# Scores of the last query chunk of images two to four in half as many products, and the second head mixing one step later

## The chip, the cores and the metric

The kernel runs on one core of a Trainium2 chip. The metric is the device time of one execution in microseconds (us). Engines are named as the profile names them: PE multiplies matrices (PEld loads its weights), DVE, ACT and POOL work on elements, SP issues most of the transfers.

## The reference, cut to what matters

```python
def _attn_ref(q, k, v, w_pre, w_post):          # 4 images, 12 heads, 448 rows, 64 wide
    scores = scale * np.matmul(q, k.transpose(0, 1, 3, 2))
    scores = np.einsum('bhij,hg->bgij', scores, w_pre)       # first mixing of heads
    scores = scores - np.max(scores, axis=-1, keepdims=True)
    attn = np.exp(scores)
    attn = attn / (np.sum(attn, axis=-1, keepdims=True) + 1e-09)
    attn = np.einsum('bhij,hg->bgij', attn, w_post)          # second mixing
    return np.matmul(attn, v)

def _moe_ref(x, w_gate, w_val, w_out, rms_g):   # x is 1792 x 768, d_ff 1536
    xn = x / np.sqrt(np.mean(x * x, axis=-1, keepdims=True) + 1e-06) * rms_g
    g = xn @ w_gate
    return g * (1.0 / (1.0 + np.exp(-g))) * (xn @ w_val) @ w_out
```

## The kernel before

The kernel has two parts, one after the other. The **attention** (`part_a`) is a loop of 92 steps, followed by some steps that finish what is left. The **gated layer** (`part_b`) is a long row of f16 products on PE. The change is in the attention alone.

The 448 query rows of an image are cut into four chunks (`NC`), and a chunk `n` (0 to 15 over the four images) into six, six, six and five steps (`PAIRS`). A step is a pair `(n, p)` and handles 20 query rows (10 in the last step of an image). Four kinds of products on PE serve it:

- **scores** (`qk_mm`, tiles `qk`, L140): 64x64 weights cut from `q`, 448 columns of `k`. One call makes the scores of two heads for the whole chunk, in four products, into two PSUM banks of `ps_q`. In `qk`, the row half of the array (which head of the pair) goes with the bank. Six calls make a chunk, and one call stands in each step until they run out. They run about a chunk and a half ahead of the steps that use them.
- ACT and DVE copy the two banks to tiles `st` (`qk_evac`, L162 and L160), and one transfer per head (`r<-st`, L179, on SP's queue) gathers the rows into `r`, where 12 heads of 5 rows stand in 60 partitions. There are three buffers `r`.
- **first mixing** (`premix`, tiles `sp`, L187): the 64x64 weights `wk_pre` on `r`, into two banks of `ps_s`. DVE takes the row maximum (`rowmax`, `nm`, L196), ACT the exponential with its row sum (`expo`, `e`, L203). `norm` adds 1e-9 (`t`, DVE, L210), takes the reciprocal (`rp`, DVE, L212) and scales the second mixing's weights with it (`wn`, POOL, L215).
- **second mixing** (`postmix`, tiles `pm`, L226): 28 products with `e` as weights and `wn` moving. In step t it works on the pair of step t-1 (`back(1)`). ACT and DVE copy its two banks into `at_all` (`evac_a`, L265 and L263).
- **attention times values** (`av_mm`, tiles `av`, L294) of finished chunk pairs, a part of 16 instructions of the trace per head pair, one or two parts in a step. ACT copies the result to `xt`, POOL squares and adds it (`x_sum`), and once per image PE sums the columns of these squares (`sq_all`, tile `pss`, L347) for the later normalization; the scores' second bank is lent for that.

Nothing is planned by a cost model: the order on each engine is that of the calls in the loop, and tables (`qk_at`, `av_at`, `jobs_at`, `last_at`) say in which step which call stands. On PE a step reads: `sp` of one half, `qk` of one bank, `sp` of the other half, `qk` of the other bank, then `pm`, then `av`. On DVE it reads: two maxima, one `st` copy, one `at_all` copy, `t`, `rp`. In steps 23 to 78 DVE also converts weights of the gated layer (`first_w`, tiles `wac`). Scores of chunk 15 end in step 84, so steps 85 to 91 have none.

Of the kernel before, what the change touches and what calls it, by code (L numbers as in the profile page):

```python
# [7 lines left out]
F32 = mybir.dt.float32  # L8
# [16 lines left out]
GROUPS = [12, 12, 12, 9]  # L25
# [26 lines left out]
def attention_moe(ctx: ExitStack, tc, q, k, v, wpre, wpost, mask, ident, wgv, wo, rms_g, out):  # L52
# [33 lines left out]
    wk_pre = cst.tile([128, 64], F32, name="wk_pre")  # L86
    wk = cst.tile([128, HR], F32, name="wk")

    msk = pro.tile([128, 2, RH], F32, name="msk", tag="ksm1")
    we = pro.tile([128, H], F32, name="we", tag="ksm2")  # L90
    wp = pro.tile([128, H], F32, name="wp", tag="ksm3")

    def load_consts():
        nc.sync.dma_start(msk.rearrange("p a r -> p (a r)"), mask)
        nc.sync.dma_start(we, wpre)
        nc.sync.dma_start(wp, wpost)

    def setup():
        nc.vector.tensor_scalar(we, we, D ** -0.5, None, ALU.mult)
        nc.vector.memset(wk_pre, 0.0)  # L100
        for i, (o, w) in enumerate(((wk_pre[:, :HR], we), (wk, wp))):
# [10 lines left out]
    def load_q(n, hp, many=3, eng=nc.gpsimd):  # L112
        b, c = divmod(n, NC)
        if not hp:
            qt[n] = pq.tile([128, H // 2, 128], F32, name=f"q{n}", tag="q", bufs=2)
        hp = slice(hp, hp + many)
        eng.dma_start(qt[n][:, hp], q[b, :, c, hp])
# [8 lines left out]
    held = []  # L126
# [7 lines left out]
    def qk_mm(n, hp):  # L134
# [6 lines left out]

        return [[lambda j=j, u=u: one(j, u) for u in range(2)] for j in range(2)]
# [8 lines left out]

    def qk_evac(n, hp, j):
        h, np_ = 2 * hp + j, PAIRS[n % NC]
        ps = qps[n, hp][j]
        if n == 0 and h < 1 or n == 1 and h < 2 * AHEAD:
            st = pro.tile([128, S], F32, name="st", tag="st", bufs=11)
        else:
            st = pq.tile([128, S], F32, name="st", tag="st", bufs=12)
        if j:
            nc.vector.tensor_copy(st, ps[:, :S])  # L160
        else:
            nc.scalar.activation(st, ps[:, :S], AF.Copy)  # L162
        for i, (lo, hi) in enumerate(((0, EARLY), (EARLY, 2 * np_)) if n == 0 else ((0, GROUPS[n % NC]),)):
            w, at_ = RH * (hi - lo), 2 * RH * lo
            if h < H - 1:
                parts = [(h, 2 * RH, at_, 2 * w)]
            else:
                parts = [(h, RH, at_, w), (64, RH, at_ + w, w)]
            for row, k_, src, many in parts:
                dst = rt[n][row : row + (k_ - 1) * GAP + 1 : GAP, lo:hi]  # L170
                if i:
                    held.append((dst, st[src : src + many]))
                else:
# [1086 lines left out]
```

## Time and profile before

| what | us |
|---|---|
| median of 3 runs | 827.72 (825.3 to 830.05) |
| the profiled execution | 822.48 |
| its span, first to last instruction | 820.6 |
| up to the first step of the attention loop | 20.1 |
| attention loop, to the first product of the gated layer | 308.5 |
| the rest | 492.0 |

In the views below, a row of the timeline gives the start in the span, the length, engine, line, operation, the tiles (written <- read), the shape and how many instructions are merged; idle time before it and what ended it stand in brackets. A fp32 product of PE stands as two instructions, so the 4 products of `sp` in a step are x8. A row of the waits gives who waited <- for whom: us in total, times, longest. A row of the stretches gives, behind the length, the busy time of PE, PEld, DVE, ACT and POOL with the number of instructions, the granted share of PE's clock, the busy share of the transfer engines and GB/s. PE's busy time says little here: an instruction counts from its start to its modelled end, and up to four run beside each other in the quarters of the array.

### The profile page before, as it was taken

How to read it: one execution, taken by the hardware profiler on the slowest of the kernel's cores; microseconds unless marked ns; L12 is line 12 of the kernel's file. 1: busy time of each engine (PE TensorE's matmuls, PEld its weight loads, DVE VectorE, ACT ScalarE, POOL GpSimd, SP SyncE). 2: the span in 40 equal slices, each digit the busy share in tenths (PEclk: the TensorE clock that was granted, in tenths of full speed). 3: DMA queues.
4: the chain of work that ended last, by engine and by line, in shares of the span. 5: the costliest groups of instructions: out<-in, count | busy, mean ns of one | idle time of the engine just before them, and what ended most of it. 6: DMA issues, size and time to landing. Idle time of an engine off the chain costs nothing.

```text
span 820.6 us, 26914 instructions
## 1 busy us (share of the span) xinstructions
PE 794.4 (97%) x10806; PEld 485.2 (59%) x10806; DVE 634.5 (77%) x1322; ACT 507.3 (62%) x1133; POOL 350.4 (43%) x467
## 2 busy tenths in 40 slices
PE   7899999999999989899999999999999999999998
PEld 2567777767776767655555555555555555555555
DVE  5777878888798867888788978997889676547562
ACT  3677778777776867664344454545444546969850
POOL 7212343454355435843624433426144359452310
PEclk9999999999999999999999999999999999999999
DMA  7777777777876754564255644754546446566641
GB/s 216 208 216 217 219 229 222 228 219 232 222 234 200 211 147 150 158 230 118 66 177 150 183 129 127 216 149 121 174 145 201 133 127 184 157 199 176 184 135 67
DMA packets 81902, 145.15 MB, mean 177 GB/s; under 512 B 10527, under 2 KB 72797, under 8 KB 81779
## 3 DMA queue, kind: packets, MB, share of 16 engines
q1 hardware_dynamic: 79982, 139.83, 57.0%
q0 software_dynamic: 832, 2.06, 1.0%
q8 instruction: 85, 1.39, 0.7%
q10 hardware_dynamic: 965, 1.56, 0.6%
q14 instruction: 38, 0.31, 0.1%
HBM read 72.83 MB, written 31.88 MB: 128 GB/s over the span
## 4 chain that ended last, share of the span: by engine, by line
PE 86%; DMA 8%; DVE 2%; issue 1%; ACT 1%; POOL 1%; SPq 0%; ACTq 0%; DVEq 0%; POOLq 0%
PE qk L140 7%; PE pm L226 7%; PE sp L187 7%; PE av L294 6%; PE pg L750 6%; PE pg L752 6%; PE pv L752 6%; PE pg L751 6%; PE pv L751 6%; PE pv L750 6%; DMA r<-st 6%; PE po L751 6%; PE po L750 6%; PE po L752 6%; DMA wraw<-in_wgv 1%
## 5 line engine op out<-in xcount | busy, mean ns | idle before, releaser
L187 PE MATMUL sp<-r,wk_pre 64*64 64x448 f32 x720 | 167.4, 542 | 5.4 <-DMA r<-st 3.5
L203 ACT ACTIVATE e<-sp,nm 128x448 f32<-128x448 f32 x180 | 114.3, 637 | 84.8 <-DVE nm L196 82.4
L140 PE MATMUL qk<-k,q 64*64 64x448 f32 x768 | 152.6, 559 | 5.9 <-DMA q<-in_q 4.1
L196 DVE TENSOR_REDUCE nm<-sp 128x1 f32<-128x448 f32 x180 | 110.3, 620 | 44.1 <-PE sp L187 27.4
L215 POOL TENSOR_SCALAR wn<-wk,rp 128x60 f32<-128x60 f32 x180 | 59.5, 345 | 181.8 <-DVE rp L212 109.7
L226 PEld LDWEIGHTS pm<-wn,e 60*64 60x64 f32 x5040 | 106.1, 134 | 37.6 <-POOL wn L215 23.8
L226 PE MATMUL pm<-wn,e 60*64 60x60 f32 x5040 | 106.7, 220 | 4.2 <-issue 4.1
L798 POOL TENSOR_TENSOR sg<-sg,u 128x448 f32<-128x448 f32 x36 | 45.9, 1275 | 151.2 <-ACT sg L795 106.7
L294 PE MATMUL av<-at_all,v 64*64 64x240 f32 (+6 forms) x1728 | 93.6, 316 | 4.6 <-issue 2.6
L750 PE MATMUL pv<-x,wh 128*128 128x448 f16 x264 | 93.0, 352 | 0.0
L752 PE MATMUL pv<-x,wl 128*128 128x448 f16 x264 | 93.0, 352 | 0.0
L752 PE MATMUL pg<-x,wl 128*128 128x448 f16 x264 | 93.0, 352 | 0.0
L751 PE MATMUL pv<-x,wh 128*128 128x448 f16 x264 | 93.0, 352 | 0.0
L751 PE MATMUL pg<-x,wh 128*128 128x448 f16 x264 | 93.0, 352 | 0.0
L750 PE MATMUL pg<-x,wh 128*128 128x448 f16 x264 | 93.0, 352 | 0.0
L750 PE MATMUL po<-h,fac 128*128 128x448 f16 (+1 forms) x258 | 89.8, 348 | 0.0
L751 PE MATMUL po<-h,fac 128*128 128x448 f16 (+1 forms) x258 | 89.8, 348 | 0.0
L752 PE MATMUL po<-h,fac 128*128 128x448 f16 (+1 forms) x258 | 89.8, 348 | 0.0
L750 PEld LDWEIGHTS <-wh 128*128 128x128 f16 x528 | 51.7, 98 | 48.2 <-issue 0.2
L751 PEld LDWEIGHTS <-wh 128*128 128x128 f16 x528 | 51.7, 98 | 48.3 <-issue 0.3
L752 PEld LDWEIGHTS <-wl 128*128 128x128 f16 x528 | 51.7, 98 | 48.2
L187 PEld LDWEIGHTS sp<-r,wk_pre 64*64 64x64 f32 x720 | 60.3, 133 | 27.2 <-ACT e L203 13.2
(167 smaller groups left out, 1567.3 us busy)
## 6 DMA issues: line engine op xcount, KB each, us to landing
r<-st SPq DMA_DIRECT2D x117, 210.0 KB
hraw<-td SPq DMA_DIRECT2D x84, 224.0 KB
wraw<-in_wgv SPq DMA_DIRECT2D x20, 768.0 KB
td<-keep SPq DMA_DIRECT2D x48, 224.0 KB
wraw<-in_wo SPq DMA_DIRECT2D x12, 768.0 KB
r<-st SPq DMA_DIRECT2D x44, 157.5 KB
v<-in_v SPq DMA_DIRECT2D x24, 256.0 KB
k<-in_k SPq DMA_DIRECT2D x24, 224.0 KB
```

The lines of the kernel that those rows point to most:

```text
L140: nc.tensor.matmul(ps[j][m, :S], qt[n][sl, hp, m], kt[n // NC, hp][sl], start=True, stop=True)
L187: nc.tensor.matmul(o, wk_pre[sl], rt[n][sl, 2 * p + v_], start=True, stop=True)
L196: nc.vector.tensor_reduce(t, ps[:, :S], AX.X, ALU.max, negate=True)
L203: nc.scalar.activation(e, ps[:, :S], AF.Exp, bias=nmx.pop((n, p, u)), accum_out=sm[n, p][:, u : u + 1])
L215: nc.gpsimd.tensor_scalar(wn[n, p][:, u], wk, r[:, u : u + 1], 1.0, ALU.mult, ALU.mult)
L226: nc.tensor.matmul(o[:, :, at_], e_[sl, j : j + JT], w_[sl].rearrange("p (s i) -> p s i", s=2), start=True, stop=True)
L294: nc.tensor.matmul(x, vt[b, hp][sl, j, c_], a, start=(c_ == 0), stop=(c_ == JC - 1))
L750: nc.tensor.matmul(ps, a, xh[:, kk, at_], start=(kk == 0), stop=False)
L751: nc.tensor.matmul(ps, a, xl_[:, kk, at_], start=False, stop=False)
L752: nc.tensor.matmul(ps, a2, xh[:, kk, at_], start=False, stop=(kk == KT - 1))
L798: nc.gpsimd.tensor_tensor(h, sg, u, ALU.mult)
```

## The change

- In images two to four the fourth chunk (chunks 7, 11, 15; `shared`) has fewer rows of its own: the other three chunks carry 8 rows of it each, in the 8 places of 128 that they had free, and the fourth keeps 60 rows per head. Its scores take three calls instead of six, each for four heads with 64 rows. The four products of a call are the same in size; two of them, of the two row halves, now write the same bank.
- The scores' schedule is compressed: a chunk starts one step after the chunk two before it has begun. Steps 34, 35, 57, 58 and 80 to 84 have no scores now.
- The `st` tiles become one tile `st_all` of 12 parts (`st_1` for chunk 1). After every third call (half a chunk) a small transfer (`rest_out`) takes the extra rows to a new tile `rest`, 12 rows of four stored per half chunk in place of the gather; a shared chunk issues four at once, of 12 rows each. The first and the last step of a shared chunk read `rest` with a second set of weights `wk_pre[:, 1]`.
- The second mixing stands two steps behind the first, up to step 84; step 85 makes two of them, and from there on it is one step behind as before. The values products start one step later with it, up to chunk 11.
- In `norm`, adding 1e-9 goes from DVE to POOL (except for the last chunk).
- The column sums of images one to three move from steps 40, 63 and 84 to steps 57, 79 and 84.

```diff
-    for i, a in enumerate([(n, hp) for n in range(1, NCHUNK) for hp in range(H // 2)][AHEAD:]):
-        qk_at[i].append(a)
+    starts, t_ = {}, -1
+    for n in range(1, NCHUNK):
+        for hp in range(H // 4 if shared(n) else H // 2):
+            if n == 1 and hp < AHEAD:
+                continue
+            t_ = max(t_ + 1, first[n - 2] + 1 if n > 1 else 0)
+            starts.setdefault(n, t_)
+            qk_at[t_].append((n, hp))
+    mix_at = [[] for _ in range(T + 40)]
+    near = first[14] + 4
+    for i, step in enumerate(steps):
+        mix_at[i + 2 if i < near - 2 else max(i + 1, near)].append(step)
...
+        def two(j, i):
+            sl, u = slice(64 * j, 64 * j + 64), (i + j) % 2
+            nc.tensor.matmul(ps[i][64 * u : 64 * u + 64, :S], qt[n][sl, 2 * hp + i], kt[n // NC, 2 * hp + i][sl], start=True, stop=True)
+
+        if shared(n):
+            return [[lambda j=j, i=i: two(j, i) for j in (i, 1 - i)] for i in range(2)]
...
+    def rest_out(n, half, st):
+        if shared(n):
+            for i in range(2):
+                for u in range(2):
+                    rows = slice(100 + 12 * u, 112 + 12 * u)
+                    nc.sync.dma_start(rest[rows, slot(n - 3 + i)], st[64 * u + 60 + 2 * i : 64 * u + 62 + 2 * i, :6])
+        else:
+            nc.sync.dma_start(rest[4 + half : 4 + half + 95 : 2, slot(n)], st[120:, 6 * half : 6 * half + 6])
...
-        nc.vector.tensor_scalar(t, s, 1e-9, None, ALU.add)
+        (nc.gpsimd if n < NCHUNK - 1 else nc.vector).tensor_scalar(t, s, 1e-9, None, ALU.add)
...
-        t = first[NC * b + NC + 2] + (5 if b < B - 2 else 3)
-        for i in range(17):
-            last_at[t + max(i - 2, 0) // 3].append((sq_all, b, i))
-        chain(t, lambda b=b: x_scale_ops(b), 2 if b < B - 2 else 4)
+        t = (first[10] - 1, first[13] + 4, first[14] + 3)[b]
+        for i in range(16):
+            last_at[t + (max(i - 1, 0) if i < 4 else 3 + (i - 4) // 3)].append((sq_all, b, i))
+        chain((first[6] + 8, first[10] + 6, first[14] + 3)[b], lambda b=b: x_scale_ops(b), 1 if b < B - 2 else 4)
...
-            if back(1):
-                postmix(*back(1))
+            for a in mix_at[t]:
+                postmix(*a)
+                if a is not mix_at[t][-1]:
+                    for v_ in range(2):
+                        evac_a(*a, v_)
```

PE in steps 34 and 35 before (the last step of chunk 5 and the first of chunk 6; `qk` are scores of chunk 7):

```order
L187 MATMUL sp<-r_123,wk_pre 64x448 x2
L140 MATMUL qk<-k_3_1036,q_2195 64x448 x2
L187 MATMUL sp<-r_123,wk_pre 64x448 x2
L140 MATMUL qk<-k_3_1036,q_2195 64x448 x2
L226 MATMUL pm<-wn,e 64x2x30 x28
L294 MATMUL av<-at_all,v_2_1337 64x220 x8
L187 MATMUL sp<-r_121,wk_pre 64x448 x2
L140 MATMUL qk<-k_4_1104,q_2195 64x448 x2
L187 MATMUL sp<-r_121,wk_pre 64x448 x2
L140 MATMUL qk<-k_4_1104,q_2195 64x448 x2
L226 MATMUL pm<-wn,e 64x2x30 x28
```

And PE in the same two steps now, up to the first product of step 36:

```order
L232 MATMUL sp<-r_126,wk_pre 64x448 x4
L271 MATMUL pm<-wn,e 64x2x30 x28
L339 MATMUL av<-at_all,v_1_1099 64x220 x4
L339 MATMUL av<-at_all,v_1_1099 64x2x55 x4
L232 MATMUL sp<-r_124,wk_pre 64x448 x4
L271 MATMUL pm<-wn,e 64x2x30 x28
L339 MATMUL av<-at_all,v_2_1251 64x220 x8
L232 MATMUL sp<-r_124,wk_pre 64x448 x2
```

The eight score products are gone from the two steps, and the values products stand one step later.

PE in steps 84 and 85 before, the fourth and fifth of chunk 14, with the column sums of image three at the end of step 84:

```order
L187 MATMUL sp<-r_123,wk_pre 64x448 x2
L140 MATMUL qk<-k_5_5062,q_6111 64x448 x2
L187 MATMUL sp<-r_123,wk_pre 64x448 x2
L140 MATMUL qk<-k_5_5062,q_6111 64x448 x2
L226 MATMUL pm<-wn,e 64x2x30 x28
L294 MATMUL av<-at_all,v_2_6272 64x240 x12
L294 MATMUL av<-at_all,v_2_6272 64x2x60 x4
L347 MATMUL pss<-ones,sum_5224 112x1 x4
L187 MATMUL sp<-r_123,wk_pre 64x448 x4
L226 MATMUL pm<-wn,e 64x2x30 x28
L294 MATMUL av<-at_all,v_3_6429 64x240 x12
L294 MATMUL av<-at_all,v_3_6429 64x2x60 x4
```

And PE in the same two steps now:

```order
L232 MATMUL sp<-r_126,wk_pre 64x448 x4
L271 MATMUL pm<-wn,e 64x2x30 x28
L339 MATMUL av<-at_all,v_1_5881 64x240 x4
L339 MATMUL av<-at_all,v_1_5881 64x2x60 x4
L339 MATMUL av<-at_all,v_2_6041 64x240 x8
L392 MATMUL pss<-ones,sum_5109 112x1 x4
L232 MATMUL sp<-r_126,wk_pre 64x448 x4
L271 MATMUL pm<-wn,e 64x2x30 x56
L339 MATMUL av<-at_all,v_2_6041 64x240 x4
L339 MATMUL av<-at_all,v_2_6041 64x2x60 x4
L339 MATMUL av<-at_all,v_3_6199 64x240 x12
L339 MATMUL av<-at_all,v_3_6199 64x2x60 x4
```

Step 85 now has two second mixings in a row, which write the same two banks, and three parts of values products behind them.

DVE in one step of image two before, from one pair of maxima to the next:

```order
L196 TENSOR_REDUCE nm<-sp 128x1 x2
L160 COPY st<-qk 128x448
L263 COPY at_all<-pm 128x2x42x5
L210 TENSOR_SCALAR t<-s 128x2
L212 RECIPROCAL rp<-t 128x2
```

DVE in such a step now, with the conversion that follows it there:

```order
L241 TENSOR_REDUCE nm<-sp 128x1 x2
L194 COPY st<-qk 128x448
L308 COPY at_all<-pm 128x84x5
L257 RECIPROCAL rp<-t 128x2
L622 TENSOR_SCALAR wac<-wac 128x384
```

And POOL now, over two steps there:

```order
L255 TENSOR_SCALAR t<-s 128x2
L260 TENSOR_SCALAR wn<-wk,rp 128x60 x2
L363 TENSOR_TENSOR xt_3206<-xt_3206,xt_3207 128x480
L255 TENSOR_SCALAR t<-s 128x2
L260 TENSOR_SCALAR wn<-wk,rp 128x60 x2
```

The addition `t` left DVE for POOL, where it stands behind POOL's own sum of the step.

## Rows read from the trace of the kernel before

**Rows 1.** Stretches: loop without values, loop with, its end, gated layer.

```profile
20.10:60.60 40.50, 37.70 (x876) 24.60 (x877) 29.91 (x74) 28.46 (x73) 8.84 (x27) 1.00 0.74 212
60.60:288.00 227.40, 219.07 (x5876) 170.60 (x5877) 189.01 (x506) 171.03 (x468) 98.30 (x214) 1.00 0.76 221
288.00:328.60 40.60, 37.58 (x1028) 28.23 (x1021) 29.65 (x89) 28.12 (x75) 20.13 (x45) 1.00 0.50 146
340.00:820.60 480.60, 476.33 (x2701) 249.67 (x2698) 365.32 (x623) 267.13 (x492) 199.08 (x151) 1.00 0.51 156
```

**Rows 2.** Timeline of PE in steps 32 and 33, with scores.

```profile
125.84 0.54 PE L187 MATMUL sp<-r,wk_pre 64*64 64x448 f32 x1
...
129.10 0.54 PE L187 MATMUL sp<-r,wk_pre 64*64 64x448 f32 x1
...
130.60 1.01 PE L226 MATMUL pm<-wn,e 60*64 60x60 f32 x51
...
131.98 0.54 PE L187 MATMUL sp<-r,wk_pre 64*64 64x448 f32 x1
```

**Rows 3.** Timeline of DVE in the same two steps.

```profile
127.86 0.63 DVE L196 TENSOR_REDUCE nm<-sp 128x1 f32<-128x448 f32 x1 [0.27 <-PE sp L187]
128.40 0.61 DVE L160 COPY st<-qk 128x448 f32<-128x448 f32 x1
...
129.44 0.16 DVE L210 TENSOR_SCALAR t<-s 128x2 f32<-128x2 f32 x1
129.70 0.17 DVE L212 RECIPROCAL rp<-t 128x2 f32<-128x2 f32 x1
...
131.49 0.61 DVE L160 COPY st<-qk 128x448 f32<-128x448 f32 x1
```

**Rows 4.** Timeline of PE in step 87, which has no scores.

```profile
318.23 0.97 PE L187 MATMUL sp<-r,wk_pre 64*64 64x448 f32 x8
319.03 1.08 PE L226 MATMUL pm<-wn,e 60*64 60x60 f32 x55
...
319.90 1.64 PE L294 MATMUL av<-at_all,v 64*64 64x240 f32 x31
321.32 1.00 PE L187 MATMUL sp<-r,wk_pre 64*64 64x448 f32 x8
```

**Rows 5.** Timeline of ACT in step 87: the two exponentials.

```profile
319.95 0.64 ACT L203 ACTIVATE e<-sp,nm 128x448 f32<-128x448 f32 x1 [1.36 <-DVE nm L196]
...
320.58 0.63 ACT L203 ACTIVATE e<-sp,nm 128x448 f32<-128x448 f32 x1
```

**Rows 6.** Waits: two of PE up to 330 us, and the longest of PEld.

```profile
PE pm L226 <- issue: 4.1, 5, 1.1
PE sp L187 <- DMA r<-st: 3.5, 5, 2.0
...
PEld pm L226 <- POOL wn L215: 23.8, 65, 1.1
```

**Rows 7.** Timeline of PE: first products of steps 80 and 81.

```profile
287.98 0.54 PE L187 MATMUL sp<-r,wk_pre 64*64 64x448 f32 x1
...
293.63 0.59 PE L187 MATMUL sp<-r,wk_pre 64*64 64x448 f32 x2 [0.55 <-DMA r<-st]
```

**Rows 8.** Timeline of PE: starts of steps 40 to 42, column sums between.

```profile
152.91 0.71 PE L187 MATMUL sp<-r,wk_pre 64*64 64x448 f32 x2
...
156.27 0.95 PE L347 MATMUL pss<-ones,sum 128*112 128x1 f32 x8
157.15 1.00 PE L187 MATMUL sp<-r,wk_pre 64*64 64x448 f32 x8
...
160.71 0.59 PE L187 MATMUL sp<-r,wk_pre 64*64 64x448 f32 x2
```

**Rows 9.** Groups of POOL up to 330 us: count | busy, mean ns | idle.

```profile
L318 POOL TENSOR_TENSOR xt<-xt,xt 128x480 f32<-128x480 f32 (+1 forms) x21 | 24.2, 1152 | 0.0
...
L374 POOL TENSOR_SCALAR u<-u 112x4 f32<-112x4 f32 x9 | 1.7, 193 | 0.6
```

More of the change, by code (lines that the diff above doesn't have):

```diff
@@ L24, with shared @@
 WIDE = [60, 60, 55, 50]
-GROUPS = [12, 12, 12, 9]
+SPLIT = 6
+WHOLE = 9
+def shared(n):
+    return n >= NC and n % NC == NC - 1
 SP_ = 460
@@ L150, in alone, with gather @@
         in_turn(*parts)
+    def gather(n, h, src, lo, hi, held_):
+        w, at_ = RH * (hi - lo), 2 * RH * lo
+        if h < H - 1:
+            parts = [(h, 2 * RH, at_, 2 * w)]
+        else:
+            parts = [(h, RH, at_, w), (64, RH, at_ + w, w)]
+        for row, k_, from_, many in parts:
+            dst = rt[n][row : row + (k_ - 1) * GAP + 1 : GAP, lo:hi]
+            x = src[from_ : from_ + many]
+            if held_:
+                held.append((dst, x))
+            else:
+                turn = h if row < H else h + 1
+                if n:
+                    eng = nc.gpsimd if n == 1 and 6 <= h < 2 * AHEAD else nc.sync
+                else:
+                    eng = nc.sync if turn % 2 else nc.gpsimd if turn < 6 else nc.scalar
+                eng.dma_start(dst, x)
@@ L163, in qk_evac @@
[L163 to L173, printed above, removed]
-                    turn = h if row < H else h + 1
-                    if n:
-                        eng = nc.gpsimd if n == 1 and 6 <= h < 2 * AHEAD else nc.sync
-                    else:
-                        eng = nc.sync if turn % 2 else nc.gpsimd if turn < 6 else nc.scalar
-                    eng.dma_start(dst, st[src : src + many])
+        at_ = 2 * hp + j
@@ new lines, in qk_evac @@
+        st = st_1 if n == 1 else st_all
+        if j:
+            nc.vector.tensor_copy(st[:, at_], qps[n, hp][j][:, :S])
+        else:
+            nc.scalar.activation(st[:, at_], qps[n, hp][j][:, :S], AF.Copy)
+        if j and n >= NC and hp % 3 == 2:
+            rest_out(n, hp // 3, st)
+        if shared(n):
+            for u in range(2):
+                waiting.append((n, 2 * (2 * hp + j) + (u + j) % 2, st[64 * u : 64 * u + 64, at_], 0, SPLIT, False))
+            if at_ < 3 or at_ == 5:
+                for args in waiting:
+                    gather(*args)
+                waiting.clear()
+        else:
+            for i, (lo, hi) in enumerate(((0, EARLY), (EARLY, H)) if n == 0 else ((0, H if n % NC < NC - 1 else WHOLE),)):
+                gather(n, at_, st[:, at_], lo, hi, i)
@@ L183, in premix, with rows @@
         sps[n, p] = ps
+        last = shared(n)
+        kind = int(last and p in (0, PAIRS[-1] - 1))
+        def rows(sl, i):
+            if not kind:
+                return rt[n][sl, i - 2 * last]
+            return rest[sl, slot(n - 3 + (i if p == 0 else 2))]
         def one(u, v_, o):
             sl = slice(64 * u, 64 * u + 64)
-            nc.tensor.matmul(o, wk_pre[sl], rt[n][sl, 2 * p + v_], start=True, stop=True)
+            nc.tensor.matmul(o, wk_pre[sl, kind], rows(sl, 2 * p + v_), start=True, stop=True)
         if len(ps) == 1:
@@ L427, in attention_moe @@
             for i in range(2):
-                job(6 * n - 16 + 3 * i, load_q, n, 3 * i, 3, nc.sync)
+                job(starts[n] - 5 + (1 if shared(n) else 3) * i, load_q, n, 3 * i, 3, nc.sync)
         for hp in range(H // 2):
@@ L439, in attention_moe @@
             if n % NC == NC - 1 and n + 1 < NCHUNK:
-                job(t + 1, load_k, n // NC + 1, hp)
+                for i in (2 * hp, 2 * hp + 1) if shared(n) else (hp,):
+                    job(t + 1, load_k, n // NC + 1, i)
     chains = []
```

147 lines of the change are left out of this document (84 added, 63 removed).

## The prediction, made before the changed kernel ran

> **What bounds the kernel now.** I read the stretches first, for where the change can act at all [rows 1]. The gated layer keeps PE busy for 476 of its 481 us and is not touched; the change acts in the 308.5 us of the attention loop, before it. The clock stays at full speed there.
>
> Then I asked what a step costs, on PE's timeline of two neighbouring steps [rows 2]. They take 3.26 and 2.88 us, 3.07 in the mean. In the second one PE does first mixing and scores for 1.50 us (129.10 to 130.60) and second mixing and one part of values for 1.38 us (to 131.98), without a hole. This looks like a kernel bound by PE. The stretch ahead speaks against that: the first 13 steps have hardly any values to multiply, some 0.6 us less work, and still take 40.5 / 13 = 3.1 us [rows 1]. So something else has a period of 3.1 too. DVE's timeline shows it [rows 3]: from one `st` copy to the next it is 3.09 us. The chain is: DVE copies the scores' second bank to `st`; only then may PE's next scores write that bank; the second half of the first mixing stands behind these scores on PE; DVE takes its maximum (127.86, after waiting 0.27 us for PE), and the next `st` copy stands behind that maximum. PE and this chain are about equally long, so a normal step will not fall below 3.07 by much, whatever leaves PE alone.
>
> Last I read what disturbs the steps. Steps 13 to 79 take 227.4 us, 3.39 each, that is 0.32 us above 3.07 [rows 1]. Some of this is PE waiting for the gathers (3.5 us, of which one wait of 2.0) and pauses for which the profile shows no cause (4.1 us ahead of second mixings) [rows 6]; the column sums and the end of the loop are priced below.
>
> **Scores taken out.** Three calls less in each of three images. On PE a call costs 1.50 [rows 2] less the 0.80 us of a first mixing alone (318.23 to 319.03) [rows 4], 0.70 us; nine are 6.3 us. But a step without scores has other limits. Its PE work is 0.80 + 1.38 = 2.2 us. The chain through the exponentials is longer: in step 87 the first exponential starts 1.72 us after the first mixing and takes 0.64, the second ends 2.98 us after it [rows 4, 5], and the next first mixing needs both banks back. If the halves overlap, 1.72 + 0.64 + 0.1 = 2.45 us is the period; if not, 3.09, as measured there (with twice the values). I take the middle, 2.75. Steps 34, 35, 57 and 58 then gain 4 x (3.07 - 2.75) = **1.3 us** (bounds 0 and 2.5).
>
> **The end, steps 80 to 86.** They take 318.23 - 287.98 = 30.25 us now [rows 4, 7], with a pause and late gathers in them. After the change: steps 80 to 82 have no scores and at most one part of values, 3 x 2.75 = 8.25. A part of values is 1.42 / 2 = 0.71 and a second mixing 0.87 us [rows 4]. Step 83 has three parts: 0.80 + 0.87 + 2.13 = 3.8. Step 84 has two parts and the column sums, 0.88 us (156.27 to 157.15) [rows 8]: 4.0. Step 85 has two second mixings on the same two banks. The second must wait for the copies of the first, which on ACT stand behind the step's exponentials: these end at 2.98 us, a copy of this size takes 0.61 as on DVE [rows 3], so it starts at 3.6 instead of 1.7, and 0.87 + 2.13 follow: 6.6. Step 86: 0.80 + 0.87 + 1.42 = 3.1. Sum 25.75, and 0.7 for pauses that come anyway: 26.4, a gain of **3.8 us** (bounds 2 and 6).
>
> **Column sums.** In image one they make two steps 160.71 - 152.91 = 7.80 us instead of 6.14 [rows 8]: 0.88 for the products, and then the scores of the next step wait for the borrowed bank. That is 1.66, for two images 3.3. In step 57 they will cost 2.2 + 0.88 - 2.75, some 0.4; in step 79, which has scores, 0.88 less what the free step behind it takes back, some 0.6. Gain **2.3 us** (bounds 1 and 3).
>
> **Earlier scores, gathers.** Scores of chunk 14 end in step 76 instead of 78, two steps earlier against first use, others one step or more. The gather waits behind the first (3.5 - 2.0 = 1.5 us [rows 6], half of it in the end that is already counted) go: **0.6 us**. Per chunk two small transfers are added on SP, four in a shared chunk, 30 in all. Behind them on that queue wait gathers, the next image's `k`, `q`, `v` and the stores of `xt`. Each has several steps of 3 us until its use, so I cost them at nothing; if that cover is gone, `r` comes late as at 293.63 [rows 7], half a us at each of 12 chunks, 6 us.
>
> **Second mixing later, `t` on POOL.** PEld waits 23.8 us for `wn` in 65 steps [rows 6]; PE itself shows no such wait, since the weights load beside running products. With the weights a step old this is over. DVE loses `t`, 0.26 us from start to start [rows 3]; POOL gets it at about 0.19 us, the price of its small operation [rows 9]. Both bring slack to the chain's sides, not to the chain. I take **1.5 us** (bounds 0 and 8; a loss is the third rival).
>
> The bank that two row halves now share is costed at nothing in the sum. Every row here has each row half in its own bank, so no row shows the price. The Trainium skill, TensorEngine Tiling (Array Packing), section Gotcha 1: PSUM Pressure, states that different row tiles cannot access the same PSUM bank at the same time; by it the sum would lose the second rival's price. No row of this trace shows the case.
>
> Sum: 1.3 + 3.8 + 2.3 + 0.6 + 1.5 = 9.5 us. The profiled execution took 822.48, 5.2 below the median of the runs, 827.72; the difference is taken from the median: **818 us**. (A profiled execution would be near 813.)
>
> **Rivals.**
> 1. *Normal steps shorten too.* If `wn` and `t` did hold the step, it goes from 3.07 toward the 2.88 of PE's undisturbed step [rows 2]; half of that over 65 steps is 6 us more: 812. For it: PEld's waits. Against it: 3.1 us in the first 13 steps, where PE has time to spare.
> 2. *The shared bank.* If the two products of a score call that write one bank can't run beside each other, a call lengthens by up to half of the 1.50 us phase, 0.75; the nine shared calls cost 6.8 us: 825. For it speaks only that the old order keeps row halves in banks of their own. Against: the other two products of a phase fill the quarters meanwhile.
> 3. *DVE waits for POOL, slower.* The reciprocal stands behind `t`, now on POOL, and the next maxima behind the reciprocal. POOL's row sum of the step (1.15 us) [rows 9] stands ahead of `t`. It costs from the point where the reciprocal starts more than 0.27 us later than now, which is DVE's slack at 127.86 [rows 3]; at half a us it is 0.23 x 87 = 20 us, less the 2 us that DVE saves at other places: 836. Against: two `wn`, the sum and `t` need some 2 us of POOL's 3.07.
> 4. *Little gained.* Steps without scores stay at 3.09 and the pauses of PE move into the denser steps, whose instructions follow each other faster: 1.3 + 1 us and three pauses of 1 us lost, 824.
>
> **Chances.** Forecast (814 to 822) 0.50, rival 1 0.15, rival 2 0.12, rival 4 0.13, rival 3 0.10. The range 810 to 826 leaves out rival 3 and the ends. A measurement of this kernel can tell about 0.5%, 4.1 us, from no change: faster means below 823.6. Faster: 0.50 + 0.15 and half of rivals 2 and 4, 0.77; same 0.14; slower 0.09.
>
> **What would show it.** Right: in the changed kernel's timeline steps 34, 35, 57, 58 last 2.5 to 3.0 us and normal steps 3.07; steps 80 to 86 some 26 us with a hole of 2 us in step 85; PEld no longer waits for POOL; no PE wait for `r` behind step 3. Wrong: normal steps at 2.9 (rival 1); phases of first mixing and scores in steps 31 to 33 above 1.5 us (rival 2); DVE's reciprocal waiting for POOL ahead of late maxima (rival 3); PE waiting for gathers or pausing more often than before (rival 4, or the small transfers' cover gone).

## The result, and the profile after

The changed kernel takes **836.1 us** (median of 4 runs, 835.04 to 841.2) beside 828.88 for the kernel before in the same session: ratio 1.0127, interval 1.0085 to 1.0169. Seven later runs (e17) gave 838.54 and 1.0104 (1.0063 to 1.0146). It is slower by 1.0 to 1.3%. The ratios leave out single slow executions and the medians do not, so a ratio is not the quotient of two medians. The prediction was 818 us with a range of 810 to 826: wrong in sign.

The profiled execution took 835.04 us, its span is 833.1, 12.5 us more than before. The stretches of the changed kernel, answering [rows 1] (columns as there):

```profile
20.20:60.85 40.65, 38.35 (x818) 24.46 (x820) 28.47 (x60) 27.90 (x72) 12.30 (x40) 1.00 0.73 210
60.85:296.62 235.77, 224.91 (x5854) 180.34 (x5844) 181.22 (x434) 170.47 (x467) 111.26 (x271) 0.99 0.73 216
296.62:341.67 45.05, 39.19 (x1033) 29.64 (x1032) 24.85 (x78) 25.23 (x68) 22.98 (x61) 0.89 0.35 106
352.00:833.10 481.10, 476.21 (x2698) 249.47 (x2696) 364.19 (x622) 266.38 (x491) 199.58 (x150) 1.00 0.51 156
```

The start and the gated layer are as before. Steps 13 to 79 take 8.4 us more (235.77 against 227.4), the end 4.5 more (45.05 against 40.6), and there the granted clock is 0.89. PE's waits in the attention, answering [rows 6]:

```profile
PE qk L149 <- DMA q<-in_q: 4.5, 2, 4.1
PE av L339 <- issue: 4.2, 4, 1.4
PE qk L149 <- issue: 3.5, 1, 3.5
PE pm L271 <- issue: 3.3, 5, 1.7
PE sp L232 <- ACT e L248: 2.4, 7, 0.7
...
PE av L339 <- ACT xt L349: 1.7, 1, 1.7
PE pm L271 <- ACT at_all L310: 1.3, 1, 1.3
PE sp L232 <- DMA r<-st: 0.5, 2, 0.3
```

The late gathers are gone, as forecast (0.5 us for 3.5), though the kernel before has only 0.9 us of them in its second profile (e16). In their place stand one wait of scores (3.5), one of values (1.7) and one of the second mixing (1.3). From the starts of the first mixings one reads which steps are long: step 37 takes 9.87 us, steps 84 and 85 take 7.65 and 8.89. Together they are 17 us above three normal steps.

**Step 37.** PE's timeline; behind the first half of the first mixing PE stands still for 3.5 us:

```profile
143.05 0.91 PE L232 MATMUL sp<-r,wk_pre 64*64 64x448 f32 x3
147.47 1.79 PE L149 MATMUL qk<-k,q 64*64 64x448 f32 x8 [3.51 <-issue]
```

The wait is called "issue" because PE is released by a copy that was late itself. DVE's timeline at that place shows the copy of the scores of step 36 out of their bank:

```profile
146.75 0.62 DVE L194 COPY st<-qk 128x448 f32<-128x448 f32 x1 [4.20 <-DMA rest<-st]
```

It waited 4.20 us for a small transfer. SP's own queue tells why that was late (start of the issue, length, how many):

```profile
139.59 2.06 SPq L116 DMA_DIRECT2D k<-in_k  x2
141.76 2.71 SPq L215 DMA_DIRECT2D rest<-st  x4
144.51 5.67 SPq L184 DMA_DIRECT2D r<-st  x7
```

The data of the four small transfers were complete after step 33, at 132 us. SP came to them at 141.76, since it issues one transfer after the other almost without a gap: from 128 to 153 us it waits 1.7 us for data in all, where in the kernel before it waits 10.7 us in the same stretch. They read parts 0 to 5 of `st_all`; the next chunk's first scores, in step 36, want to write parts 0 and 1. After the hole the clock is at its lower level, here and at the end (stretches of the changed kernel):

```profile
147.40:150.80 3.40, 3.33 (x31) 1.71 (x34) 1.33 (x4) 2.04 (x7) 1.19 (x3) 0.50 0.37 103
314.00:324.00 10.00, 8.74 (x152) 6.43 (x152) 3.20 (x9) 2.35 (x7) 1.03 (x5) 0.53 0.01 2
```

Half of 3.4 us and 0.47 of 10 us are 6.4 us of PE's time; the lower level lasts 0.9 us beyond the second stretch, which makes 6.8.

**Steps 84 and 85.** PE's timeline:

```profile
309.58 1.09 PE L232 MATMUL sp<-r,wk_pre 64*64 64x448 f32 x8
...
311.27 0.83 PE L339 MATMUL av<-at_all,v 64*64 64x240 f32 x15
313.76 1.96 PE L339 MATMUL av<-at_all,v 64*64 64x240 f32 x16 [1.66 <-ACT xt L349]
315.65 1.65 PE L392 MATMUL pss<-ones,sum 128*112 128x1 f32 x8
317.23 1.77 PE L232 MATMUL sp<-r,wk_pre 64*64 64x448 f32 x8
318.78 1.76 PE L271 MATMUL pm<-wn,e 60*64 60x60 f32 x56
321.81 1.81 PE L271 MATMUL pm<-wn,e 60*64 60x60 f32 x56 [1.26 <-ACT at_all L310]
```

and ACT's beside it:

```profile
312.12 0.62 ACT L248 ACTIVATE e<-sp,nm 128x448 f32<-128x448 f32 x1
...
312.73 0.52 ACT L310 ACTIVATE at_all<-pm 128x420 f32<-128x420 f32 x1
313.13 1.03 ACT L349 ACTIVATE xt<-av 128x480 f32<-128x480 f32 x2
```

Step 84 finishes one pair of values banks and starts the next in the same banks. The copy that frees them (`xt`) stands on ACT behind both exponentials and `at_all`. PE waits 1.66 us, falls to the lower clock, and works at it through the column sums and most of step 85: the second mixing takes 1.76 us instead of 1.08 [rows 4]. The forecast hole in step 85 is there, 1.26 us.

### The profile page after: what moved, and what is told of

It is laid out like the page before. It is cut to its first block, busy times and chain, and to the rows that moved or that the text cites. A ratio compares the mean times of both kernels' runs of the same rounds, so it can differ in the third digit from the quotient of the medians.

```text
span 833.1 us, 26725 instructions
## 1 busy us (share of the span) xinstructions
PE 801.2 (96%) x10734; PEld 495.1 (59%) x10734; DVE 618.1 (74%) x1224; ACT 502.6 (60%) x1124; POOL 371.8 (45%) x556
## 4 chain that ended last, share of the span: by engine, by line
PE 88%; DMA 5%; issue 2%; DVE 2%; ACT 1%; SPq 1%; POOL 0%; ACTq 0%; DVEq 0%
PE pm L271 9%; PE sp L232 8%; PE av L339 7%; PE qk L149 7%; PE pg L807 6%; PE pg L809 6%; PE pv L808 6%; PE pv L809 6%; PE pv L807 6%; PE pg L808 6%; PE po L808 6%; PE po L807 6%; PE po L809 6%; DMA r<-st 1%; DMA wraw<-in_wgv 1%
## 5 line engine op out<-in xcount | busy, mean ns | idle before, releaser
L232 PE MATMUL sp<-r,wk_pre 64*64 64x448 f32 x684 | 157.2, 549 | 3.4 <-ACT e L248 2.4
L271 PEld LDWEIGHTS pm<-wn,e 60*64 60x64 f32 x5040 | 117.5, 136 | 31.4 <-issue 13.5
L149 PE MATMUL qk<-k,q 64*64 64x448 f32 x624 | 118.1, 565 | 11.1 <-DMA q<-in_q 4.5
L271 PE MATMUL pm<-wn,e 60*64 60x60 f32 x5040 | 113.7, 222 | 5.5 <-issue 3.8
L339 PE MATMUL av<-at_all,v 64*64 64x240 f32 (+6 forms) x1728 | 96.2, 317 | 5.9 <-issue 4.2
L339 PEld LDWEIGHTS av<-at_all,v 64*64 64x64 f32 x1728 | 72.2, 134 | 9.9 <-issue 6.5
```

Of the source, the lines that this page charges most:

```text
L149: nc.tensor.matmul(ps[j][m, :S], qt[n][sl, hp, m], kt[n // NC, hp][sl], start=True, stop=True)
L232: nc.tensor.matmul(o, wk_pre[sl, kind], rows(sl, 2 * p + v_), start=True, stop=True)
L271: nc.tensor.matmul(o[:, :, at_], e_[sl, j : j + JT], w_[sl].rearrange("p (s i) -> p s i", s=2), start=True, stop=True)
L339: nc.tensor.matmul(x, vt[b, hp][sl, j, c_], a, start=(c_ == 0), stop=(c_ == JC - 1))
```

## The experiments

Edits are relative to the changed kernel unless said otherwise. In the table, "ratio" is against the kernel before in the same session; the next columns are from each run's profile: steps 36 to 38 and 57 to 60 (behind the first two shared chunks), steps 79 to 86, and PE time lost to the lower clock from the loop's start to 14 us behind its end (sum over stretches of 1 us of one less the granted share).

| run | median us | ratio (interval) | 36–38 | 57–60 | 79–86 | clock |
|---|---|---|---|---|---|---|
| before | 828.88 | 1 | 10.29 | 15.77 | 33.13 | 1.7 |
| after | 836.1 | 1.0127 (1.0085–1.0169) | 17.30 | 15.21 | 36.56 | 6.8 |
| e17, after again | 838.54 | 1.0104 (1.0063–1.0146) | 11.85 | 22.09 | 36.60 | 10.2 |
| e1 parts turned | 836.07 | 1.0104 (1.0071–1.0137) | 9.95 | 14.17 | 35.01 | 1.7 |
| e2 switch in step 81 | 833.29 | 1.0092 (1.005–1.0133) | 12.59 | 18.28 | 31.53 | 3.4 |
| e3 lag of one | 832.91 | 1.0066 (1.0023–1.0109) | 15.97 | 16.05 | 29.48 | 1.7 |
| e4 = e1 + e2 | 829.18 | 1.0071 (1.0031–1.0111) | 12.46 | 17.54 | 32.70 | 3.4 |
| e6 = e4 + own maxima | 830.81 | 1.0073 (1.0038–1.0108) | 12.43 | 16.02 | 31.27 | 0.0 |
| e12 = e6, no small transfers | 822.41 | 0.9952 (0.9918–0.9986) | 10.10 | 14.09 | 32.33 | 5.1 |
| e15 = e6, 18 of the 30 | 828.0 | 0.9995 (0.9958–1.0032) | 10.82 | 14.64 | 32.17 | 5.1 |
| e13 = e6, q on POOL | 829.32 | 1.0026 (1.0001–1.0052) | 10.56 | 16.08 | 31.33 | 6.8 |
| e11 = e6, lag of one | 830.41 | 1.0037 (1.0002–1.0071) | 10.64 | 21.89 | 29.43 | 8.5 |
| e14 = e11, q on POOL | 826.76 | 0.999 (0.9952–1.0029) | 10.64 | 17.84 | 29.36 | 1.7 |

The kernel before moves between sessions too (825.2 to 828.9), so the ratios are what to compare. Single executions of one kernel lie up to 18 us apart, which the last section takes up.

**e1, the release of `st_all`.** Chunks 8 to 11 use the parts turned by six (`turned(n)` is 6 there and 0 elsewhere):

```diff
-        st = st_1 if n == 1 else st_all
+        st, x_ = st_1 if n == 1 else st_all, (at_ + turned(n)) % H
...
+        a = (6 * half + turned(n)) % H
...
-            nc.sync.dma_start(rest[4 + half : 4 + half + 95 : 2, slot(n)], st[120:, 6 * half : 6 * half + 6])
+            nc.sync.dma_start(rest[4 + half : 4 + half + 95 : 2, slot(n)], st[120:, a : a + 6])
```

> The changed kernel, and chunks 8 to 11 use the twelve parts of st_all turned by six (6 to 11, then 0 to 5), so that the first scores behind a shared chunk no longer write the parts that its small transfers still read. Number and order of all instructions stay. Theory A, release of st_all: step 37, 9.87 us in the changed kernel, falls to 3.1 to 3.5 us with its wait of 3.5 us and the half clock behind it gone, and step 60 from 4.77 to about 4.0; 836 - 6.5 - 0.7 = 829 us. Rival, the issues of SP alone hold the loop, whichever part they read: the wait only moves to the next late gather, step 37 or a neighbour stays 3 us or more too long, 833 to 836 us.

Step 37 fell from 9.87 to 3.94 us and the lower clock behind it is gone. But this profile alone does not show that the release was the cause: here SP issues the four small transfers 3.5 us before step 36 begins (at 142.28), where in the changed kernel it came to them 3.2 us after that, and so the copies of steps 36 and 37 had nothing to wait for anyway:

```profile
138.74 3.09 SPq L219 DMA_DIRECT2D rest<-st  x4
```

```profile
144.72 0.61 DVE L194 COPY st<-qk 128x448 f32<-128x448 f32 x1
```

The run e4 (below), which has the same turn of the parts, settles it. There SP is as late as in the changed kernel, 3.2 us behind the start of step 36 (138.47), and the copy of that step's scores does not wait: it begins while SP is still issuing the small transfers.

```profile
141.63 2.91 SPq L219 DMA_DIRECT2D rest<-st  x4
```

```profile
143.43 0.61 DVE L194 COPY st<-qk 128x448 f32<-128x448 f32 x1
```

In all four profiles without the turn (after, e17, e2, e3) the copies of steps 37 and 60 wait, 0.7 to 4.2 us; in the profiles with it none of them waits over 0.6 us. So the release is the cause of the long step. But the median of e1 stayed at 836.07, where 829 was expected; the rival's number fits that better. Taking one wait away did not make the kernel measurably faster.

**e17, the changed kernel again**, for a second profile.

> The changed kernel, unchanged. If its three long steps come from its order and not from chance, they are there again (37 about 10 us, 84 and 85 about 16 together) and the time is 836 within 2; if they were chance, the steps are short and the time under 832.

Steps 84 and 85 are there again (7.09 and 9.49). The wait for `st_all` stands behind the next shared chunk this time, in step 60 (9.21 us; step 37 takes 5.45). PE and DVE there:

```profile
232.07 1.95 PE L149 MATMUL qk<-k,q 64*64 64x448 f32 x8 [2.88 <-issue]
```

```profile
231.34 0.62 DVE L194 COPY st<-qk 128x448 f32<-128x448 f32 x1 [3.57 <-DMA rest<-st]
```

**e2, the switch of the lag in step 81** (values of chunks 12 and 13 start in step 82, a head pair in each step):

```diff
-    near = first[14] + 4
+    near = first[14]
```

> The changed kernel, but the step from two steps of lag to one is made in step 81 (two second mixings in step 81, which has no scores) and not in step 85; the values of chunks 12 and 13 start in step 82, a whole head pair in each step. Theory: the loss at the end comes from step 84, where a part of values opens the banks whose copy still stands behind the exponentials, from the double mixing in step 85, and from the half clock that follows the hole; steps 80 to 86 fall from 32.5 us to 25 to 27 us and the clock stays at full speed there: 836 - 6 = 830 us. Rival: the end is limited by the chain from the first mixing through exponentials in each step without scores, 3.1 us a step and more with two parts of values; steps 80 to 86 take 30 us as before the change, 833 to 834 us.

Steps 80 to 86 took 27.47 us for 32.49, with the full clock in all of it, though the double mixing keeps a hole of 1.80 us in step 81. The theory on the end holds for these steps. The median fell by 2.8 us instead of 6, and the ratio (1.0092) cannot be told from that of e1 or of the changed kernel. This profile had its long step at the next place, step 60 with 7.30 us, and another, step 64 with 7.42, behind a pause of 3.2 us.

**e3, a lag of one throughout** (the lines that start the values one step earlier again are left out here):

```diff
-        mix_at[i + 2 if i < near - 2 else max(i + 1, near)].append(step)
+        mix_at[i + 1].append(step)
```

> The changed kernel with the second mixing one step behind the first throughout, as before the change, and the values products as early as then. It tells what the two steps of lag bring by themselves. Theory: normal steps are held by the chain of scores, copy, first mixing and maximum, and gain nothing from the lag; they stay at 3.07 to 3.15 us, and the end gets back to one head pair of values in a step: 836 - 6 = 830 us, as with the lag of two and the switch in step 81. Rival, that the lag does help: steps 13 to 79 become 3 us or more longer than in the changed kernel, 833 us or above.

832.91, beside 833.29 with two steps of lag (e2), in ratios 1.0066 beside 1.0092. The lag brings nothing that can be measured.

**e4, e1 and e2 together.**

> Both repairs together: parts of st_all turned by six for chunks 8 to 11, and the lag switched in step 81. If both losses are separate, they add up: 836 - 7 - 6 = 823 us, which is under the kernel before (828). If the pauses of PE for its instructions take their place, 826 to 829 us.

829.18, by medians 7 us under the changed kernel, by ratios 0.3 to 0.6% (3 to 5 us), and 1.0071 of the kernel before, not under it. In this profile the scores wait for `k` in step 36 (1.55 us) and for `q` in step 39 (1.53), other transfers of the same queue, and once more in step 59 (1.22 us, put down to an operation of DVE that the scores do not read). The hole of the double mixing in step 81 (1.80 us) is followed by the lower clock here.

**e5, e6 and e7, the addition on POOL.** The order of the instructions shows what the addition did on DVE: it waited for ACT in each step. Without it, the maximum has to make sure itself that ACT has read an older maximum whose place it takes. The trace bears this out. In the kernel before 176 of the 180 maxima on record wait for one semaphore, PE's; in the changed kernel 149 of 177 wait for two, and a wait instruction of DVE stands ahead of each of these; in e6 174 of 177 wait for one again.

e5 is e4 with the addition on DVE, e6 is e4 with a column of its own for each maximum, e7 is the kernel before with the addition on POOL:

```diff
-            t = nmx[n, p, u] = pe.tile([128, 1], F32, name="nm", tag="nm")           # e6
+            t = nmx[n, p, u] = nm_all[:, (c_ := 2 * steps.index((n, p)) + u) : c_ + 1]
...
-        nc.vector.tensor_scalar(t, s, 1e-9, None, ALU.add)                           # e7, in before
+        (nc.gpsimd if n < NCHUNK - 1 else nc.vector).tensor_scalar(t, s, 1e-9, None, ALU.add)
```

> Both repairs of the last run (parts of st_all turned, lag switched in step 81), and the addition of 1e-9 back on DVE. In the changed kernel DVE's maximum waits for two semaphores, PE's and ACT's, since DVE no longer waits for ACT in the step through the addition; an extra wait instruction stands in front of each maximum, and from the last product of the first mixing to the maximum it takes 0.64 us where the kernel before takes 0.57, in the chain that sets the step. Theory: with the addition on DVE the normal step goes from 3.13 back to 3.06 us (steps 7 to 10 show it, without values products): 70 steps by 0.06 = 4 us less than the run before, 825 us. Rival, POOL's addition costs nothing in the chain and DVE's own costs 0.26 us of DVE a step: 829 us or more.

> Both repairs, the addition stays on POOL, but the row maxima get a place of their own for each step (184 columns of one tile) so that no maximum has to wait for ACT to have read an older one; the extra wait instruction is gone. If the extra wait is what the move of the addition costs, the normal step is 3.06 us here as well and the time 825 us. If the place of the addition costs (the reciprocal waits for POOL), steps stay at 3.13 and the time at 829.

> The kernel before with one line of the change: the addition of 1e-9 on POOL for chunks 0 to 14. Theory: steps 7 to 10 go from 3.06 to 3.13 us, and the time rises by 80 steps by 0.06 = 5 us, 831 us beside 826. Rival, as the forecast had it: POOL has time to spare, DVE gets 0.26 us a step, no change or a gain of a microsecond: 825 to 826 us.

Step by step the theory holds. From the last products of the first mixing to the maximum it takes 0.68 us in e7 and 0.60 in e6 (0.61 before). PE and DVE of e7:

```profile
50.97 0.57 PE L187 MATMUL sp<-r,wk_pre 64*64 64x448 f32 x2
```

```profile
51.65 0.62 DVE L196 TENSOR_REDUCE nm<-sp 128x1 f32<-128x448 f32 x1 [0.57 <-PE sp L187]
```

and of e6:

```profile
50.65 0.57 PE L236 MATMUL sp<-r,wk_pre 64*64 64x448 f32 x2
```

```profile
51.25 0.62 DVE L247 TENSOR_REDUCE nm_all<-sp 128x1 f32<-128x448 f32 x1 [0.51 <-PE sp L236]
```

Steps 9 and 10, without values products, are 3.13 us long in the changed kernel, in e4 and in e7, and 3.06 in the kernel before and in e6. In the time this hardly shows: e7 825.76 beside 825.16, ratio 1.003 (0.9997 to 1.0062), where 831 was expected; e6 830.81; e5 831.37, 1.0081 (1.0039 to 1.0123; its profile is of an execution of 4573 us and is not used). Probably the later steps are held by PE's own work, by waits or by pauses more often than by this chain, so that 0.07 us of it are paid in few of them; no run shows that by itself.

**e12, the small transfers left out** (with them the extra rows of the shared chunks, so that the first and last steps of these chunks work on zeros):

```diff
-        if j and n >= NC and hp % 3 == 2:
-            rest_out(n, hp // 3, st)
```

> Three repairs (831 us), and the 30 small transfers left out, so the extra rows of the shared chunks are not computed (the first and last steps of these chunks work on zeros). Theory, the small transfers and what waits behind them on SP's queue cost some 5 us: 826 us. Rival, the gathers and k of the shared chunk come in three steps with or without them: 829 to 831 us.

This is the largest step of all: 830.81 to 822.41, in ratios 1.0073 to 0.9952, 1.2% or 10 us, and under the kernel before. The two intervals do not touch. PE's waits in e6 (the rows on scores and gathers, and the longest):

```profile
PE pm L277 <- issue: 3.1, 5, 1.6
...
PE qk L149 <- DMA k<-in_k: 1.5, 1, 1.5
PE sp L236 <- DMA r<-st: 1.3, 4, 0.5
PE qk L149 <- DVE nm_all L247: 0.9, 1, 0.9
...
PE qk L149 <- DVE st L194: 0.7, 1, 0.7
PE qk L149 <- DMA q<-in_q: 0.7, 1, 0.7
PE qk L149 <- DVE wac L627: 0.7, 1, 0.7
```

and in e12, where no score waits for anything any more (4.5 us in e6, about half of the gain; e1's profile shows no such wait either, so these waits alone do not make a kernel's time):

```profile
PE av L343 <- issue: 4.9, 3, 3.6
PE pm L275 <- issue: 4.7, 8, 1.6
...
PE sp L234 <- DMA r<-st: 0.3, 1, 0.3
```

How far SP runs ahead of its data can be read from its own waits between 60 and 300 us. The row of the gathers that wait beside ACT's `at_all`, the largest before, here before, changed, and in e12:

```profile
SPq L179 <- ACT at_all L265: 35.2, 29, 4.0
```

```profile
SPq L184 <- ACT at_all L310: 10.8, 15, 1.4
```

```profile
SPq L184 <- ACT at_all L314: 30.3, 28, 2.5
```

A queue that waits for data has time to spare. With the small transfers, 24 of these 35 us are gone; without them most are back. All rows together go from 113.6 to 80.6 us (84.6 in e6), and to 100.1 in e12. So SP has time left in the sum; it has almost none behind a shared chunk, where from 128 to 153 us 1.7 of 10.7 us are left.

**e15, only the 12 of the shared chunks left out:**

```diff
-        if j and n >= NC and hp % 3 == 2:
+        if j and n >= NC and hp % 3 == 2 and not shared(n):
```

> Three repairs (831 us), with the 12 small transfers of the shared chunks left out and the 18 others kept (a part of the extra rows is then zero). If the burst behind the shared chunks is what costs, the time is as without any small transfer, 823 us; if all 30 cost alike, 8.4 x 12 / 30 = 3.4 us are gained, 827 to 828 us.

828.0, ratio 0.9995: by medians 2.8 of the 8.4 us, by ratios 0.8 of the 1.2%. The twelve cost something clear of the noise (the intervals of e6 and e15 do not touch). That the other 18 cost as well is likely, but the intervals of e15 and e12 overlap, and how the two groups share the cost is not settled.

**e13 and e14, the loads of `q` taken off SP**, with two steps of lag and with one (e11):

```diff
-                job(starts[n] - 5 + (1 if shared(n) else 3) * i, load_q, n, 3 * i, 3, nc.sync)
+                job(starts[n] - 5 + (1 if shared(n) else 3) * i, load_q, n, 3 * i, 3, nc.gpsimd)
```

> Three repairs (831 us), with the 23 loads of q in the loop issued by POOL instead of SP; they wait for no work of the same step. Theory, SP's issuing time is what the small transfers cost: 14 us of issues leave SP for the 21 that the small transfers brought, two thirds of the 8 us come back, 825 to 827 us, and k is in time in steps 36 and 59. Rival, it is the small transfers' own waits and landing times, not SP's time: 830 us or above.

> Parts of st_all turned and own places for the maxima, and one step of lag throughout, as before the change; against the run with three repairs (831 us) this tells what two steps of lag bring. Theory, they bring nothing, since PE loads the weights of the second mixing beside running products: 831 us within 1.5, and without the double mixing in step 81 (a hole of 1.8 us) 1 to 2 us less, 829. Rival, they save the 1.5 us that the forecast gave them and more: 833 us or above.

> As e13, but with one step of lag throughout (without a double second mixing): 1 to 2 us less than e13, 824 to 826 us, if SP's time is what costs; 829 us or above otherwise.

By ratios, taking these 14 us of issues off SP gave 0.47% in both pairs (1.0073 to 1.0026, 1.0037 to 0.999), about 4 us, some 40% of what the small transfers cost. That is less than the two thirds expected, and in each pair the two intervals overlap; the direction, twice the same, is that of the theory. What the rest goes through (the small transfers' landing, or the number in flight) stays open. One step of lag instead of two gave 0.36% in both pairs, within overlapping intervals too. e14 is the best version with the whole computation, equal to the kernel before.

**Other ways to relieve SP were worse.** e8 is e5 and e10 is e6 with the small transfers issued by POOL and by ACT (`nc.gpsimd`, `nc.scalar` for `nc.sync` in `rest_out`), e9 is e6 with the calls of a shared chunk in every second step, and e18 is e14 with the loads of `k` on POOL:

```diff
-            t_ = max(t_ + 1, first[n - 2] + 1 if n > 1 else 0)                                  # e9
+            t_ = max(t_ + (2 if shared(n) and hp else 1), first[n - 2] + 1 if n > 1 else 0)
...
-        (nc.sync if b else nc.sync).dma_start(t, k[b, :, hp])                                   # e18
+        (nc.gpsimd if b else nc.sync).dma_start(t, k[b, :, hp])
```

> As the run with both repairs and the addition on DVE, but the 30 small transfers are issued by POOL instead of SP. In the changed kernel SP issues without a pause from 126 to 150 us, behind the shared chunk, and k and q of the next image come late in three of the runs. Theory, SP's queue still costs: PE's waits for k, q and st in steps 35 to 40 and 58 to 61 (1.5 us each with the half clock behind them) go, some 3 to 5 us less than the run with SP's queue, 820 to 822 us. Rival, POOL's own issues cost as much, or the waits are gone already: 825 us or more.

> Three repairs (831 us), with the 30 small transfers issued by ACT instead of SP. Theory, SP's 21 us for these issues are the burden: steps 36 to 39 and 59 to 62 lose their waits, as they did with POOL's queue, without POOL's part in the step: 826 to 828 us. Rival, ACT is in the chain of the step (0.24 to 0.48 us between its exponentials are free) and an issue holds it for 0.6 us or more: 831 us or above.

> Three repairs (parts of st_all turned, lag switched in step 81, own places for the maxima; 831 us) and the three score calls of a shared chunk in every second step instead of three steps in a row, so that SP has six steps for their 12 gathers, four small transfers and 12 k. Same work. In the repaired kernel's trace steps 36, 39, 59 and 62 still last 4.5 to 5.3 us, with PE's scores waiting for k and q. Theory, SP's burst behind the shared chunk is what is left: these steps fall to 3.1 to 3.8, 831 - 5 = 826 us or less. Rival, the k and q are late for another reason (their buffers come free late): the waits stay, 830 us or more.

> As e14 (parts of st_all turned, one step of lag, own places for the maxima, q loads on POOL; 826.8 us), with the loads of k of images two to four on POOL as well. Theory, k comes late because it stands on SP's queue behind the shared chunk's gathers: steps 36 and 59 get to 3.1 to 3.9 us, 824 to 825 us, under the kernel before. Rival, POOL holds its own step up at these loads, or the waits move to another transfer: 827 us or above.

e8: 834.98 (ratio 1.0113); steps 36 to 38 are at 10.35 as expected, and others got longer, among them step 17 with 6.75 us and step 75 with 6.91. e10: 900.16, 1.0897; steps 18, 34, 42, 51, 57 and 65 take 9.4 to 11.1 us, and PE waits for gathers (up to 4.1 us), for `q` (up to 4.3) and, in the second mixing, for ACT (up to 2.9); why these transfers come so much later was not followed up. e9: 835.8, 1.0112; `k` for the third call's heads is now loaded two steps later, and PE waits 3.05 and 3.37 us for it. e18: 831.83, 1.0045, by 0.55% worse than e14 (the intervals overlap), and not better, as had been expected.

**e16, the kernel before again.**

> The kernel before, unchanged, for a second profile. If PE's pauses come from where the instructions lie in memory, they stand at the same steps as in the first profile (22, 28, 34, 57, 58, 68, 71, 80, 81); if they come from what the transfer engines happen to do, at others, and the time differs by several us.

820.49 us. The long steps 28 (5.89), 34 (4.13) and 71 (3.77) are there again; those of steps 22 and 57 are not (3.46 and 3.51), and step 80 is 1.7 us shorter. Some long steps belong to a place in the program, others come and go.

## Why the prediction was wrong

- **The small transfers, "I cost them at nothing": this step failed.** The part on earlier scores and gathers gave the issues of 30 transfers the price zero, with 6 us if their cover were gone. It was gone; by e12 they cost 1.2%, some 10 us (8.4 by the medians). It was not `r` that came late, as that price had it: PE waits only 0.5 us for gathers in the changed kernel, and 4.6 us before score products. The price lay in rows that were to be had: an issue of this queue takes 0.4 to 0.8 us, 30 are some 21 us, twelve of them stand behind the shared chunks, and there SP had some 10 us to spare in 25 (10.7 and 10.2 behind the first two). And I followed only who waits behind them on the queue, not what they hold: the parts of `st_all` that they read. This is the long step of after and of e17.
- **The end: this step failed too.** 26.4 us were worked out for steps 80 to 86, 32.49 came, more than the 30.25 of before. Step 85's hole was foreseen with 2 us and the order of ACT as its cause. For step 84 I added up PE's products (4.0 us) and did not ask whether the second part of values opens the banks that ACT has yet to copy; it did, 1.66 us. And I left out that the clock can fall after a hole: the last 2.6 us of step 84 and most of step 85 ran at half of it.
- **Second mixing later, `t` on POOL: 1.5 us were taken, none came.** Two steps of lag are rather dearer than one, by 0.36% (e6 and e11, e13 and e14; within the noise), e2 and e3 are equal. The third rival had the right place (DVE's maximum) and a wrong reason. Its sign is there: DVE's reciprocal waits for POOL's `t` 20 times in the loop of the changed kernel, 10.3 us in all. But the maximum is late by a second semaphore, 0.07 us in the chain, and moving `t` alone (e7) costs 0.3%, with an interval from nothing to 0.6%.
- **Steps without scores: the size was right, the gain did not show.** 2.75 us were put in; undisturbed ones take 2.53 to 3.05 (2.99 in step 34, 2.74 in 58, 2.58, 3.04, 2.99 in 80 to 82). But step 35 takes 4.06, of which 0.59 is a pause, and 2.6 to 4.2 in most other profiles. So steps 34, 35 and 58 of the changed kernel take 9.79 us together, where three normal ones take 9.21; in e12 they take 8.05.
- **Column sums: mis-sized.** Steps 40 and 41 lost their 1.66 us (they take 6.21 together). But the sums cost 1.0 us in step 79 (4.08 us) instead of 0.6, and 1.4 in step 57 of e12 (4.12) instead of 0.4. Before, they cost 2.9 us (1.66 and 4.08 + 3.30 - 6.14); some 0.5 us of the forecast 2.3 is left.
- **The shared bank: close to nothing, as costed.** The second rival falls. PE of e4, a score call of a shared chunk with the two row halves in one bank (first rows) and one with a bank for each (last rows), from the first mixing's first product to the second mixing's:

```profile
125.99 0.54 PE L236 MATMUL sp<-r,wk_pre 64*64 64x448 f32 x1
...
127.49 0.31 PE L275 MATMUL pm<-wn,e 60*64 60x60 f32 x5
```

```profile
119.65 0.54 PE L236 MATMUL sp<-r,wk_pre 64*64 64x448 f32 x1
...
121.16 0.33 PE L275 MATMUL pm<-wn,e 60*64 60x60 f32 x4
```

  1.50 and 1.51 us. Over the calls of e4 in which PE stands still nowhere before the second mixing, the eight of shared chunks take 1.50 to 1.68 us, 1.64 in the middle, the others 1.55; in e14 it is 1.51 beside 1.53. That is 0.1 us a call at most, some 0.8 for nine, where the rival had 0.75 a call. (In the changed kernel steps 31 to 33 take 1.59, 1.87 and 1.68, above the 1.5 that was set as the rival's sign; in step 32 a copy waits 0.93 us for a small transfer.) Whether the two products of one bank run beside each other, the rows do not tell. The rule of the Trainium skill that the prediction weighed (TensorEngine Tiling (Array Packing), section Gotcha 1: PSUM Pressure) shows no larger cost here; these measurements decide.
- **The rivals:** none forecast what came. The one on the slower side, the third, had another mechanism; that its 836 us is the measured time is luck. And the fourth's pauses are not more than before (7.8 us beside 7.0, without the wait of step 37).

From 818 to 836 are 18 us. By the figures above, the small transfers make 8 to 10 of them, the end 6, the later mixing 1.5 and the column sums 1.8; this sum is an estimate, since e2, which repaired the end, gave back only 2.8 of its 6 us, within the noise. With the end and the release repaired and the small transfers gone (e12), the kernel is at 0.9952, 4.0 us under the kernel before. So the rest of the change is worth something (which part of it, no run separates); carrying the extra rows separately costs more than that.

## What to carry to other kernels

A small transfer is not free because it is small. On a queue that one engine issues one by one, count its issue (here 0.6 to 0.75 us) against the time for which that engine waits for data today, and do so at the place where the transfer will stand: here the sum over the loop (114 us) would have promised room that the 25 us behind a shared chunk (10.7 us) did not have. And ask of each transfer two things: who stands behind it on the queue, and whose buffer it holds until it lands.

Before adding up an engine's products in a dense step, list for each group the bank that it opens and where its release stands in the other engine's order. And when an operation leaves an engine, look at the waits that it did for those behind it: they come back as waits of their own.

## What the runs showed of the hardware that I had not expected

**PE's pauses.** The waits of PE called "issue" before second mixings and values (2.5 to 16.5 us in a profile) end 1.2 to 1.8 us after a packet of 16 KB on an instruction queue, taken to be PE's, has landed: 196 of 197 in the attention loops of 19 profiles; in e12 the longest, 3.6 us, ended 1.47 us after one. Most of the 62 to 64 such packets of a loop are followed by no wait, 3 to 18 are. The cause is inferred from this coincidence; no run took it away. The waits are different in executions of one kernel (6.7 us and 2.5 us in the two profiles of the kernel before) and hide effects of 2 or 3 us in any one profile. The Trainium skill, Runtime: NRT & Kernel Launch, section Instruction fetch mechanics, has the sequencer fetch such blocks while it executes and calls the cost mostly hidden; if the inference holds, it is not hidden here.

**The price of a hole.** PE idle for 1.66 us at 312 us was followed by a granted clock of 0.5 from 314.6 to 324.9 us, 3.5 us at 144 us by 0.5 until 150.8. The hole of the double mixing in step 81 is 1.80 to 1.83 us long in e2, e4, e6, e12, e13 and e15. In e4, e12 and e15 it was followed by a granted clock of 0.5 for 3.4 us, in e2, e6 and e13 by none. So a hole of this size can cost its own length once more (half of 3.4 us), or three times that, as in step 84, or nothing; what decides it these runs do not show.
